# Loading the second Wq quarter directly behind the first, with two x tiles and their transposes one step later

## The chip, the cores and the metric

The kernel runs on one core of a Trainium2 chip. The metric is the device time of one execution in microseconds. A figure for a kernel is the median of its runs, all with a granted TensorE clock of 1.0. The span is what the hardware profile of one execution covers; it is about 2 us shorter than the time of the same execution.

Some words used throughout: in this kernel TensorE does the matrix products and transposes and writes them to the memory called PSUM; ScalarE copies results out of PSUM (a *cast* is such a copy of a finished product into bf16); VectorE does the statistics and the normalisations. A load *lands* when its data have arrived.

## The reference

Two layers, each of windowed attention and a feed-forward block, on 2048 tokens of width 1024 in bf16:

```
for _ in range(2):
    x = x + attention(layernorm(x), wqkv, wo)      # 32 heads, window 8, dilation 2
    x = x + gelu(layernorm(x) @ w1 + b1) @ w2 + b2 # F = 3584
```

Only the very start matters for this change: the layer norm of the first 512 tokens and their product with Wq, the first third of wqkv.

## The kernel before

The kernel works in groups of 512 tokens, that is four x tiles of 128 tokens. For the first group it must fetch both x and Wq before TensorE can do anything useful, so it fetches Wq in four quarters (each two of the eight 128-row blocks of the contraction) and starts with x tiles 0 and 1 alone. I call this *the first half*: Wq for tokens 0 to 255. *The second half* is Wq for tokens 256 to 511, from x tiles 2 and 3.

```python
load_x(0, 0, 2)                                  # x tiles 0 and 1
wq_first = [wpool.tile([P, KD // 2, D], BF16, name="wt") for _ in range(2)]
for k in range(0, KD, 2):
    load_wq_piece(wq_first[k // (KD // 2)], k)   # one quarter, 512 KB
    if k < 4:
        load_x(0, 2 + k // 2, 3 + k // 2)        # x2 behind quarter 1, x3 behind quarter 2
# ... cut ...
def transpose_on_pe(xn, out, pst=None, parts=None):
    # ... cut ...
    for k in range(KD):                          # eight 128x128 transposes into PSUM
        pe(nc.tensor.transpose(pst[:, k, :], xn[:, k * P:(k + 1) * P], ident[:]))
    parts = parts or [act.copy]                  # then a copy from PSUM to xnT
    # ... cut ...
# in ln_first(), with VectorE and ScalarE held to program order
    both = psum.tile([P, 2, KD, P], BF16, name="L", bufs=1)
    # ... x tiles 0 and 1 ...
    stats(2)
    stats(3)                                     # statistics on VectorE, sqrt on ScalarE
    for tt in range(2, 4):
        first_late.append((norm(tt), xa[0][:, tt, :, :], both[:, tt - 2, :, :]))
    # ... cut ...
# in gen_qkv(), n == 0
first = {}
for kq in range(4 if n == 0 else 0):             # Wq quarters
    for c in range(6):                           # six output chunks, six PSUM accumulators
        first[c] = qkv_chunk(wq, c, xnT, first.get(c), kq * (KD // 4), (kq + 1) * (KD // 4), 0, 2)
        if (kq, c) in ((2, 5), (3, 5)):          # x2's, then x3's transposes
            for done in range(2 if kq == 3 else 0):
                act.copy(qT[:, done, 0:2 * P], first[done][:, 0:2 * P])
            transpose_on_pe(*first_late.pop(0))
for c in list(first)[2:]:
    act.copy(qT[:, c, 0:2 * P], first[c][:, 0:2 * P])
for c in range(6 if n == 0 else NCH, NCH):       # chunks 6 and 7
    ps = qkv_chunk(wq, c, xnT, t0=0, t1=2)
    act.copy(qT[:, c, 0:2 * P], ps[:, 0:2 * P])
for c in range(NCH):                             # the second half
    t0 = 2 if n == 0 else 0
    ps = qkv_chunk(wq, c, xnT, t0=t0)
    act.copy(qT[:, c, t0 * P:], ps[:, t0 * P:])
    yield
```

TensorE's order is the program's. The order on the other engines and on the load queue is chosen by a scheduler, except where the program pins it. A half of the tile `both` is 2 KB in each partition.

Of the kernel before, what the change touches and what calls it, by code (L numbers as in the profile page):

```python
# [17 lines left out]
def kernel(  # L18
# [18 lines left out]
    P = 128  # L37
# [41 lines left out]
    def acc_tile():  # L79
        return psum.tile([P, T], F32, name="acc", bufs=6)  # L80
# [23 lines left out]
    vec, act, pool, sp = InOrder(nc.vector), InOrder(nc.scalar), InOrder(nc.gpsimd), InOrder(nc.sync)  # L104
# [6 lines left out]
    def pe(inst):  # L111
        if last_pe[0] is not None:
            dep_order(inst, last_pe[0], "PE program order")
        last_pe[0] = inst
        return inst

    def mm(*args, **kwargs):
        return pe(nc.tensor.matmul(*args, **kwargs))  # L118
# [3 lines left out]
    def load_x(g, t0=0, t1=NTT):  # L122
        for tt in range(t0, t1):
            t = g * NTT + tt
            sp.dma_start(x[t][:], x_in[t * P:(t + 1) * P, :])

    def load_qkv(which):
        tiles = []
        for h in range(2):
            wt = wpool.tile([P, KD // 2, D], BF16, name="wt")  # L130
            sp.dma_start(wt[:], wqkv_v[:, h * (KD // 2):(h + 1) * (KD // 2), which * D:(which + 1) * D])
            tiles.append(wt)
        return tiles

    def load_wq_piece(wt, k):
        sp.dma_start(wt[:, k % (KD // 2):k % (KD // 2) + 2, :], wqkv_v[:, k:k + 2, 0:D])
# [2 lines left out]
    wq_first = [wpool.tile([P, KD // 2, D], BF16, name="wt") for _ in range(2)]  # L139
    for k in range(0, KD, 2):  # L140
        load_wq_piece(wq_first[k // (KD // 2)], k)
        if k < 4:
            load_x(0, 2 + k // 2, 3 + k // 2)

    warm = bigp.tile([P, P], BF16, name="big")
    vec.memset(warm[:], 0.0)
# [68 lines left out]
    def transpose_on_pe(xn, out, pst=None, parts=None):  # L215
        if pst is None:
            pst = psum.tile([P, KD, P], BF16, name="acc", bufs=6)
        for k in range(KD):
            pe(nc.tensor.transpose(pst[:, k, :], xn[:, k * P:(k + 1) * P], ident[:]))  # L219
        parts = parts or [act.copy]  # L220
        n = KD // len(parts)
        for h, copy in enumerate(parts):
            copy(out[:, h * n:(h + 1) * n, :], pst[:, h * n:(h + 1) * n, :])
# [8 lines left out]
    first_late = []  # L232
# [51 lines left out]
    def qkv_chunk(wts, c, xnT, ps=None, k0=0, k1=KD, t0=0, t1=NTT):  # L284
        if ps is None:
            ps = acc_tile()
        for k in range(k0, k1):
            mm(ps[:, t0 * P:t1 * P], lhsT=wts[k // (KD // 2)][:, k % (KD // 2), c::NCH], rhs=xnT[:, t0:t1, k, :],
               start=(k == 0), stop=(k == KD - 1), skip_group_check=t1 - t0 < NTT)
        return ps  # L290
# [16 lines left out]
    def new_prod(n, c):  # L307

        s = st[n]
        prod = bigp.tile([P, NTT, W, P], BF16, name="big")  # L310
        q = s["qT"][:, c, :].rearrange("p (b t) -> p b t", t=P)
        vec.tensor_tensor(out=prod[:], in0=q.unsqueeze(2).to_broadcast([P, NTT, W, P]), in1=win_by_tile(s["kT"][:, c, :]), op=ALU.mult)
        tree = s["prods"]
        tree.append(prod)
        if c % 2 == 1:
            for _ in range(1 if c % (NCH // s["parts"]) == 1 else 2):
                b = tree.pop()
                vec.tensor_tensor(out=tree[-1][:], in0=tree[-1][:], in1=b[:], op=ALU.add)

    def gen_qkv(n, parts=1, defer=False, qk_pool=None, v_late=False, qk_next=None):  # L320
        g = n % NG
        xnT = xa.pop(n)
        s = st[n]
        s["parts"] = parts
        s["prods"] = []
        qk_pool = qk_pool or attp
        wq = wq_first if n == 0 else load_qkv(0)
        wk = load_qkv(1)
        if n == 0:
            early_tiles = ln_early((1, None), (2, qk_next))  # L330
            for _ in range(NTT):
                next(early_tiles)
            wv = load_qkv(2)
            for _ in early_tiles:
                pass
            load_x(3)
        qT = qk_pool.tile([P, NCH, T], BF16, name="qT")
        first = {}
        for kq in range(4 if n == 0 else 0):
            for c in range(6):  # L340
                first[c] = qkv_chunk(wq, c, xnT, first.get(c), kq * (KD // 4), (kq + 1) * (KD // 4), 0, 2)
                if (kq, c) in ((2, 5), (3, 5)):
                    for done in range(2 if kq == 3 else 0):
                        act.copy(qT[:, done, 0:2 * P], first[done][:, 0:2 * P])
                    transpose_on_pe(*first_late.pop(0))
        for c in list(first)[2:]:
            act.copy(qT[:, c, 0:2 * P], first[c][:, 0:2 * P])
        for c in range(6 if n == 0 else NCH, NCH):
            ps = qkv_chunk(wq, c, xnT, t0=0, t1=2)
            act.copy(qT[:, c, 0:2 * P], ps[:, 0:2 * P])  # L350
        for c in range(NCH):
            t0 = 2 if n == 0 else 0
            ps = qkv_chunk(wq, c, xnT, t0=t0)
            act.copy(qT[:, c, t0 * P:], ps[:, t0 * P:])
            yield
        if n > 0 and not v_late:
            wv = load_qkv(2)
        kT = qk_pool.tile([P, NCH, HALO + T], BF16, name="kT")
        s["qT"], s["kT"] = qT, kT
        act.on = n > 2  # L360
        act.copy(kT[:, :, 0:HALO], (zhalo if g == 0 else khalo)[:])
        act.on = False
        for c in range(NCH):
            ps = qkv_chunk(wk, c, xnT)
            act.copy(kT[:, c, HALO:], ps[:])
            if not defer:
                new_prod(n, c)
            yield
        if g + 1 < NG:
            act.copy(khalo[:], kT[:, :, T:T + HALO])  # L370
        vT = attp.tile([P, NCH, HALO + T], BF16, name="vT", bufs=2)
        s["vT"] = vT
        if v_late:
            wv = load_qkv(2)
        act.on = n > 2
        act.copy(vT[:, :, 0:HALO], (zhalo if g == 0 else vhalo)[:])
        act.on = False
        for c in range(NCH):
            ps = qkv_chunk(wv, c, xnT)
            act.copy(vT[:, c, HALO:], ps[:])  # L380
            yield
        if g + 1 < NG:
            act.copy(vhalo[:], vT[:, :, T:T + HALO])
# [163 lines left out]
    def ln_early(*groups):  # L547

        tiles = []
        for n, pool in groups:  # L550
            xa[n] = new_xnT(pool)
            xns = bigp.tile([P, NTT, D], BF16, name="big") if pool is None else pool.tile([P, NTT, D], BF16, name="qT")
            tiles += [(n * NTT + tt, xns[:, tt, :], xa[n][:, tt, :, :]) for tt in range(NTT)]
        vec.on = True
        ahead = ln_stats(tiles[0][0])
        for i, (t, xn, xT) in enumerate(tiles):
            mv_rstd = ahead
            if i + 1 < len(tiles):
                ahead = ln_stats(tiles[i + 1][0])
            ln_norm(t, *mv_rstd, xn)  # L560
            sp.dma_start_transpose(xT, xn.rearrange("s (k p) -> s k p", p=P))
            if i + 1 == len(tiles):
                vec.on = False
            yield
# [28 lines left out]
    with tc.tile_pool(name="early", bufs=1) as early:  # L593
        load_x(1)
        load_x(2)
        stage(gen_qkv(0, qk_next=early), sides=at(14, load_b2))
        q1 = gen_qkv(1, defer=True, qk_pool=early)
        stage(q1, sides=at(6, attend, 0) + at(6, spread, 0) + at(6, hold) + each(new_prod, 1, 8, 1, 0, 4) + each(av, 0, 12, 1))
        q2 = gen_qkv(2, defer=True)
        stage(q2, 18)  # L600
        new_prod(1, 4)
        hold()
        stage(gen_wo(0))
        hold()
        stage(q2, sides=each(new_prod, 1, 0, 1, 5, 8))
# [15 lines left out]
    n = N - 2  # L621
# [35 lines left out]
```

## Time and profile before

Six runs: median 1232.87 us, 1232.72 to 1234.22 (three of them, with the median 1233.37, were known when the prediction was made). The profiled run has a span of 1230.8 us. Two lines of its page: the busy time of each engine with its share of the span, and the chain of work that ended last, by engine.

```profile
PE 1222.2 (99%) x5739; PEld 632.6 (51%) x5789; DVE 861.9 (70%) x922; ACT 307.3 (25%) x491; POOL 87.2 (7%) x207
...
PE 99%; DMA 1%; issue 0%; SPq 0%; DVE 0%
```

TensorE is the bottleneck, and the chain is TensorE nearly all the way. So a change can win only what TensorE waits, and loses whatever wait it adds. TensorE's timeline at the start shows that wait. The columns are start in us, length in us, engine, source line, operation, output and inputs, number of instructions, and in brackets the idle time before and what ended it.

```profile
8.92 2.81 PE L118 MATMUL acc<-xnT,wt 128*128 128x256 bf16 x24
12.06 1.53 PE L118 MATMUL acc<-xnT,wt 128*128 128x256 bf16 x12 [0.33 <-DMA wt<-in_A_wqkv_dram]
13.43 0.61 PE L219 MATMUL L<-ident,xn 128*128 128x128 bf16 x8
13.88 1.48 PE L118 MATMUL acc<-xnT,wt 128*128 128x256 bf16 x12
15.20 0.61 PE L219 MATMUL L<-ident,xn 128*128 128x128 bf16 x8
15.64 1.59 PE L118 MATMUL acc<-xnT,wt 128*128 128x256 bf16 x13
```

The 8.92 line is quarters 1 and 2, the 12.06 line is quarter 3 after a 0.33 us wait for its load, then x2's transposes, quarter 4, x3's transposes, and from 15.64 chunks 6 and 7 and everything after. One reading trap: a matmul of this shape is listed with 273 ns (the profile models where it ends), but the next starts 109 ns later.

VectorE in the same stretch (statistics of x2, of x3, then the two normalisations):

```profile
8.89 1.28 DVE L93 BATCH_NORM_STATS2 stats<-x 128x6 f32<-128x512 bf16 x2
...
10.69 1.29 DVE L93 BATCH_NORM_STATS2 stats<-x 128x6 f32<-128x512 bf16 x2 [0.28 <-DMA x<-in_A_x_dram]
...
12.28 0.55 DVE L93 TENSOR_SCALAR xn<-x,mv,rstd 128x1024 bf16<-128x1024 bf16 x1
...
12.94 0.55 DVE L93 TENSOR_SCALAR xn<-x,mv,rstd 128x1024 bf16<-128x1024 bf16 x1
```

ScalarE: x2's copy out of PSUM, casts of finished accumulators, x3's copy.

```profile
14.08 1.01 ACT L93 COPY xnT<-L 128x1024 bf16<-128x1024 bf16 x1 [1.11 <-PE L L219]
14.99 1.21 ACT L93 CAST qT<-acc 128x256 bf16<-128x256 f32 x4
16.04 1.07 ACT L93 COPY xnT<-L 128x1024 bf16<-128x1024 bf16 x1
```

x3's copy runs from 16.04 to 17.11 us, while TensorE works on chunks 6 and 7. By counting records, the second half starts at 17.40 us (its first matmul is the 81st record after 64 matmuls and 16 transposes, beginning with the first Wq matmul), so the copy is hidden.

### The profile page before, as it was taken

How to read it: one execution, taken by the hardware profiler on the slowest of the kernel's cores; microseconds unless marked ns; L12 is line 12 of the kernel's file. 1: busy time of each engine (PE TensorE's matmuls, PEld its weight loads, DVE VectorE, ACT ScalarE, POOL GpSimd, SP SyncE). 2: the span in 40 equal slices, each digit the busy share in tenths (PEclk: the TensorE clock that was granted, in tenths of full speed). 3: DMA queues.
4: the chain of work that ended last, by engine and by line, in shares of the span. 5: the costliest groups of instructions: out<-in, count | busy, mean ns of one | idle time of the engine just before them, and what ended most of it. 6: DMA issues, size and time to landing. Idle time of an engine off the chain costs nothing.

```text
span 1230.8 us, 13962 instructions
## 1 busy us (share of the span) xinstructions
PE 1222.2 (99%) x5739; PEld 632.6 (51%) x5789; DVE 861.9 (70%) x922; ACT 307.3 (25%) x491; POOL 87.2 (7%) x207
## 2 busy tenths in 40 slices
PE   9999999999999999999999999999999999999998
PEld 7666544456444564445544465444654444444444
DVE  7989899988998599375993759937599797011001
ACT  4343152014320143202431024310244101400310
POOL 3010010010010000100011000010000002000000
PEclk9999999999999999999999999999999999999999
DMA  9954665656556654856447565486664558446441
GB/s 290 300 179 143 182 222 185 201 154 209 181 165 215 180 162 163 229 172 186 150 163 238 171 171 170 158 223 202 171 196 145 188 196 208 151 158 196 155 135 52
DMA packets 219391, 225.06 MB, mean 183 GB/s; under 512 B 68194, under 2 KB 187136, under 8 KB 217024
## 3 DMA queue, kind: packets, MB, share of 16 engines
q1 hardware_dynamic: 214704, 208.69, 55.5%
q0 software_dynamic: 4624, 15.49, 3.3%
q8 instruction: 45, 0.74, 0.2%
q14 instruction: 18, 0.15, 0.0%
HBM read 191.11 MB, written 4.72 MB: 159 GB/s over the span
## 4 chain that ended last, share of the span: by engine, by line
PE 99%; DMA 1%; issue 0%; SPq 0%; DVE 0%
PE acc L118 98%; DMA wt<-in_A_wqkv_dram 1%; SPq L93 0%; PE L L118 0%; PE L L219 0%; DVE x L93 0%
## 5 line engine op out<-in xcount | busy, mean ns | idle before, releaser
L118 PE MATMUL acc<-xnT,wt 128*128 128x512 bf16 (+1 forms) x3392 | 720.9, 375 | 0.4 <-DMA wt<-in_A_wqkv_dram 0.3
L118 PEld LDWEIGHTS <-wt 128*128 128x128 bf16 x3392 | 400.5, 119 | 319.1 <-issue 1.4
L118 PE MATMUL acc<-wt,hT 128*128 128x512 bf16 (+1 forms) x1780 | 386.0, 376 | 2.1
L118 PEld LDWEIGHTS <-hT 128*128 128x128 bf16 x1820 | 178.1, 98 | 208.9
L93 DVE TENSOR_TENSOR big<-big 128x1024 bf16<-128x1024 bf16 (+2 forms) x184 | 245.2, 1360 | 2.2
L93 ACT ACTIVATE hT<-acc,b1T 128x512 bf16<-128x512 f32 x224 | 152.7, 688 | 332.3 <-PE acc L118 332.1
L93 DVE TENSOR_TENSOR big<-qT,kT 128x4096 bf16<-128x4096 bf16 x64 | 143.8, 2286 | 48.4 <-ACT kT L93 47.8
L93 DVE TENSOR_TENSOR big<-abc,vT 128x4096 bf16<-128x4096 bf16 x64 | 144.7, 2286 | 14.0 <-DMA abc<-a 13.4
L93 DVE TENSOR_TENSOR tmp<-acc,b2bc 128x512 f32<-128x512 f32 x56 | 38.6, 690 | 146.7 <-PE acc L118 143.7
L93 ACT CAST qT<-acc 128x512 bf16<-128x512 f32 (+1 forms) x72 | 38.0, 545 | 351.1 <-PE acc L118 351.1
L118 PE MATMUL acc<-wt,oT 128*128 128x512 bf16 x440 | 97.4, 379 | 0.4
L93 DVE BATCH_NORM_STATS2 stats<-x 128x6 f32<-128x512 bf16 x128 | 85.6, 682 | 4.5 <-DMA x<-in_A_x_dram 3.4
L118 PEld LDWEIGHTS <-oT 128*128 128x128 bf16 x448 | 43.8, 98 | 52.8
L93 DVE TENSOR_TENSOR x<-acc,big 128x512 bf16<-128x512 f32 (+1 forms) x9 | 5.7, 633 | 90.0 <-PE acc L118 90.0
L93 ACT CAST vT<-acc 128x512 bf16<-128x512 f32 x64 | 37.5, 586 | 83.3 <-PE acc L118 83.3
L93 ACT CAST kT<-acc 128x512 bf16<-128x512 f32 x64 | 37.4, 587 | 67.0 <-PE acc L118 67.0
L93 POOL TENSOR_TENSOR rstd<-mv,eps_t 128x1 f32<-128x1 f32 x56 | 14.2, 253 | 515.4 <-DVE mv L93 509.4
L93 DVE TENSOR_TENSOR x<-acc,x 128x512 bf16<-128x512 f32 x64 | 42.9, 671 | 4.8 <-PE acc L118 4.4
L93 DVE TENSOR_SCALAR xn<-x,mv,rstd 128x1024 bf16<-128x1024 bf16 x52 | 28.4, 547 | 20.2 <-POOL rstd L93 20.1
L93 DVE TENSOR_TENSOR x<-tmp,x 128x512 bf16<-128x512 f32 x56 | 38.7, 690 | 1.3
L93 POOL DMA_DIRECT2D big<-big x24 | 13.3, 565 | 256.3 <-DVE big L93 237.6
L93 POOL TENSOR_TENSOR rstd<-rstd,mhalf 128x1 f32<-128x1 f32 x56 | 31.0, 553 | 4.4
(68 smaller groups left out, 228.8 us busy)
## 6 DMA issues: line engine op xcount, KB each, us to landing
wt<-in_B_w_dram SPq DMA_DIRECT2D x56, 1024.0 KB, 5.7
wt<-in_B_w_dram SPq DMA_DIRECT2D x64, 896.0 KB, 4.9
wt<-in_A_wqkv_dram SPq DMA_DIRECT2D x46, 1024.0 KB, 5.6
wt<-in_A_wo_dram SPq DMA_DIRECT2D x16, 1024.0 KB, 5.0
big<-big POOLq DMA_DIRECT2D x24, 256.0 KB, 3.6
abc<-a POOLq DMA_DIRECT2D x24, 256.0 KB, 5.3
x<-in_A_x_dram SPq DMA_DIRECT2D x16, 256.0 KB, 6.2
out_dram<-x SPq DMA_DIRECT2D x31, 128.0 KB, 2.1
```

Source lines behind the costliest of these rows:

```text
L93: inst = f(*args, **kwargs)
L118: return pe(nc.tensor.matmul(*args, **kwargs))
```

## The change

The intent is to remove the wait for quarter 3: quarter 2 is loaded directly behind quarter 1, x2 and x3 move one quarter back in the queue, and since they land later, their transposes move back too: x2's into the middle of quarter 4, x3's behind chunks 6 and 7.

```diff
     for k in range(0, KD, 2):
         load_wq_piece(wq_first[k // (KD // 2)], k)
-        if k < 4:
-            load_x(0, 2 + k // 2, 3 + k // 2)
+        if 0 < k < 6:
+            load_x(0, 1 + k // 2, 2 + k // 2)
@@
                 first[c] = qkv_chunk(wq, c, xnT, first.get(c), kq * (KD // 4), (kq + 1) * (KD // 4), 0, 2)
-                if (kq, c) in ((2, 5), (3, 5)):
-                    for done in range(2 if kq == 3 else 0):
-                        act.copy(qT[:, done, 0:2 * P], first[done][:, 0:2 * P])
+                if (kq, c) == (3, 2):
                     transpose_on_pe(*first_late.pop(0))
-        for c in list(first)[2:]:
+        for c in list(first)[:3]:
             act.copy(qT[:, c, 0:2 * P], first[c][:, 0:2 * P])
         for c in range(6 if n == 0 else NCH, NCH):
-            ps = qkv_chunk(wq, c, xnT, t0=0, t1=2)
-            act.copy(qT[:, c, 0:2 * P], ps[:, 0:2 * P])
+            first[c] = qkv_chunk(wq, c, xnT, t0=0, t1=2)
+        if n == 0:
+            transpose_on_pe(*first_late.pop(0))
+        for c in list(first)[3:]:
+            act.copy(qT[:, c, 0:2 * P], first[c][:, 0:2 * P])
```

## The prediction

> **What bounds the kernel.** TensorE. The page gives PE busy 1222.2 of 1230.8 us (99%), and the chain of waits is 98% the matmul helper. It touches only the first 18 us, where a merged timeline shows three PE waits: 1.05 us for the memset, 1.50 us for the first normalised tile (matmuls resume at 7.15), and 0.33 us for the third Wq quarter (11.73 to 12.06). The first two stay. After 12.06 no PE wait is listed, so PE time won or lost before reaches the end unabsorbed.
>
> **What changes.** Nothing is added or removed: same matmuls, transposes, copies, DMAs, reordered. Landings before (issue plus time to landing): Wq quarter 1 at 7.9, x2 8.6, quarter 2 10.0, x3 10.7, quarter 3 12.0, quarter 4 13.35 us. They land in issue order, about 0.67 us per x tile and 1.35 per quarter. That agrees with the Trainium skill, "DMA: Bandwidth & Descriptors", section "Two DMAs through the same engine are not ordered": descriptors of one queue start in order but are pipelined. Estimated landings after: quarter 2 9.3, x2 10.0, quarter 3 11.35, x3 12.0, quarter 4 still 13.35.
>
> PE after, by 0.114 us per 128x256 matmul step:
> - Quarters 1 and 2 run 8.92 to 11.7, quarter 3 without a wait to 13.1: the 0.33 us wait is gone.
> - PE then waits about 0.25 us for quarter 4 (13.35). The wait is moved, not removed.
> - DVE runs in program order and normalises x2 only after the statistics of x3, which start at 12.05 instead of 10.69 us; xn2 is ready at 14.2 (before 12.83). PE reaches x2's transposes after six matmuls at 14.05: another 0.15 us wait.
> - Transposes (0.45), six matmuls, 16 matmuls of chunks 6 and 7: to about 17.2; x3's transposes to 17.65.
> - The next instruction, the first matmul over token tiles 2 and 3, reads all of xnT tile 3, which ScalarE still has to copy out of PSUM. Before, chunks 6 and 7 (1.83 us of PE) stood between and hid the copy; now nothing does. PSUM drain and semaphore 0.2 to 0.4, copy 1.01 to 1.07 us in the trace. ScalarE's order also puts chunk 7's qT cast (0.37 us) ahead of it. PE waits about 1.5 us (17.65 to 19.15).
>
> Sum, all critical: -0.33 +0.25 +0.15 +1.5, about +1.6 us (first matmul of the second half at 17.47 before, about 19.1 after).
>
> **Prediction.** 1233.37 + 1.6 = about 1235.0 us; 8 in 10: 1233.4 to 1236.6. Runs of before spread by 1.3 us. Faster by over 2%: 0.005; within 2%: 0.985; slower by over 2%: 0.01.
>
> **What would show it right or wrong.** A PE wait of 1.2 to 1.8 us released by ScalarE's xnT copy near 17.7; no wait at quarter 3; a wait of 0.1 to 0.4 at quarter 4; x2's stats starting near 10.0 and x3's near 12.0; quarter 4 landing still near 13.35; DVE's start on x4 moving from 14.07 to about 14.8, harmless since PE moves more; the span past 20 us otherwise equal, shifted.
>
> **What would make it wrong.** ScalarE slower to reach x3's copy (casts stacking behind the late square root and x2's copy), up to +1 us more; a PE wait for a free accumulator at chunk 6; landings that don't follow bytes in issue order; another chip's base; a wait further on, invisible now, that absorbs the shift (then about 1233.4), or a DVE shift of 0.7 us reaching a head sum.

## The result, and the profile after

Median 1234.30 us of six runs (1233.88 to 1234.89), against 1232.87 before: +1.4 us. The ratio of the mean time of the changed kernel's fast runs to that of the fast runs of before in the same rounds is 1.001, with an interval of 0.9997 to 1.0023. (Ratios are computed so throughout, so they are not quite the ratios of the medians.) The interval includes 1, so the times alone show no difference. The traces do, one profiled run of each kernel. The span is 1232.2 us.

TensorE's timeline after, answering to the one above:

```profile
8.79 4.13 PE L118 MATMUL acc<-xnT,wt 128*128 128x256 bf16 x36
13.45 0.88 PE L118 MATMUL acc<-xnT,wt 128*128 128x256 bf16 x6 [0.52 <-DMA wt<-in_A_wqkv_dram]
14.26 0.62 PE L219 MATMUL L<-ident,xn 128*128 128x128 bf16 x8
14.71 2.57 PE L118 MATMUL acc<-xnT,wt 128*128 128x256 bf16 x22
17.12 0.61 PE L219 MATMUL L<-ident,xn 128*128 128x128 bf16 x8
18.83 5.40 PE L118 MATMUL acc<-xnT,wt 128*128 128x256 bf16 x48 [1.10 <-ACT xnT L93]
```

The first line now is quarters 1, 2 and 3 without a break: the wait for quarter 3 is gone. Quarter 4 is split in two by x2's transposes (14.26), and is waited for (0.52). Chunks 6 and 7 come before x3's transposes (17.12). Then TensorE stands still until 18.83. All waits of TensorE in the whole run, with total, number and longest:

```profile
PE acc L118 <- ACT xnT L93: 1.1, 1, 1.1
PE acc L118 <- DVE big L93: 1.1, 1, 1.1
PE acc L219 <- DVE xn L93: 0.7, 1, 0.7
PE acc L118 <- DMA wt<-in_A_wqkv_dram: 0.5, 1, 0.5
```

The two waits in the middle are the start-up (the kernel before has them too, 1.1 and 1.5 us). The first is new, and the last, for quarter 4, stands in place of the 0.3 us for quarter 3. VectorE and ScalarE, the same pieces as above:

```profile
10.03 1.29 DVE L93 BATCH_NORM_STATS2 stats<-x 128x6 f32<-128x512 bf16 x2 [1.18 <-DMA x<-in_A_x_dram]
...
12.06 1.28 DVE L93 BATCH_NORM_STATS2 stats<-x 128x6 f32<-128x512 bf16 x2 [0.50 <-DMA x<-in_A_x_dram]
...
13.65 0.55 DVE L93 TENSOR_SCALAR xn<-x,mv,rstd 128x1024 bf16<-128x1024 bf16 x1
```

```profile
15.04 1.03 ACT L93 COPY xnT<-L 128x1024 bf16<-128x1024 bf16 x1
...
17.32 0.37 ACT L93 CAST qT<-acc 128x256 bf16<-128x256 f32 x1 [0.16 <-PE acc L118]
17.77 1.01 ACT L93 COPY xnT<-L 128x1024 bf16<-128x1024 bf16 x1
```

x3's statistics start at 12.06 instead of 10.69 us, and since VectorE was told to do them before x2's normalisation, x2's is done at 14.20 instead of 12.83 us. x3's copy runs from 17.77 to 18.78, and TensorE resumes 0.05 us later.

The idle time in brackets counts from the listed end of the last matmul, so it is about 0.16 us less than what TensorE lost. Start to start, TensorE lost 0.68 us at quarter 4, 0.10 us at x2's transposes and 1.26 us behind x3's: 2.04 us, against 0.49 before. That is 1.55 us more between the first Wq matmul and the second half. In this profile the first Wq matmul came 0.13 us earlier (8.79 for 8.92), because x0, the first load of all, landed 0.13 us earlier (3.42 for 3.54 us); nothing in the change explains that. 1.55 less 0.13 is 1.42 us, and the spans differ by 1.4. From the second half's first matmul to the last matmul both kernels take the same, 1210.06 and 1210.05 us. So the whole result lies in these ten microseconds.

This gives a sharper measure than the time. For each run I quote, from the records of its profile: the start of the first Wq matmul, the start of the second half, the difference of the two (called *the stretch*), and *the rest*, from there to the start of the last matmul.

| kernel | first Wq matmul | second half | stretch | rest | span | median time | before, same rounds |
|---|---|---|---|---|---|---|---|
| before | 8.92 | 17.40 | 8.48 | 1210.06 | 1230.8 | 1232.87 | |
| changed | 8.79 | 18.83 | 10.04 | 1210.05 | 1232.2 | 1234.30 | 1232.87 |
| loads_only | 8.90 | 18.15 | 9.25 | 1210.11 | 1231.6 | 1233.53 | 1232.90 |
| places_only | 9.06 | 18.25 | 9.18 | 1210.05 | 1231.6 | 1233.94 | 1232.90 |
| x3_before_chunks | 9.07 | 18.59 | 9.52 | 1210.06 | 1232.0 | 1234.10 | 1232.90 |
| copy_in_four | 8.82 | 18.02 | 9.20 | 1210.30 | 1231.6 | 1233.82 | 1232.90 |
| casts_behind | 8.94 | 18.20 | 9.26 | 1210.17 | 1231.7 | 1233.76 | 1232.95 |
| norm2_first | 9.35 | 19.53 | 10.18 | 1210.17 | 1233.0 | 1235.00 | 1232.95 |
| loads_norm2 | 8.98 | 18.66 | 9.68 | 1210.86 | 1232.8 | 1234.42 | 1232.95 |
| x3_later_norm2 | 8.92 | 17.09 | 8.17 | 1210.37 | 1230.8 | 1232.97 | 1232.95 |
| two_tiles | 8.96 | 18.05 | 9.09 | 1210.25 | 1231.6 | 1233.69 | 1232.85 |
| best2 | 8.96 | 16.89 | 7.93 | 1211.44 | 1231.7 | 1233.33 | 1232.85 |
| loads_norm2_pool | 8.91 | 18.00 | 9.09 | 1211.02 | 1232.3 | 1234.48 | 1232.85 |
| best3 | 9.10 | 17.03 | 7.93 | 1210.39 | 1230.7 | 1232.85 | 1233.12 |

Read it with care: the first Wq matmul starts anywhere from 8.79 to 9.35 us. In all fourteen profiles it starts 5.37 to 5.38 us after x0 lands, so this spread is the spread of one landing (3.42 to 3.97 us), which no edit touches. When loads land late in a run, the waits for them grow as well, and there is one profile of each kernel. The twelve experiments ran beside runs of the kernel before. Single runs of that kernel spread from 1232.23 to 1234.63 us. A difference in time below about half a us says nothing here; a wait in the trace with its releaser does.

### The profile page after: what moved, and what is told of

Its sections match the earlier page's. It is cut to its first block, busy times and chain, and to the rows that moved or that the text cites. A ratio compares the mean times of both kernels' runs of the same rounds, so it can differ in the third digit from the quotient of the medians.

```text
span 1232.2 us, 13962 instructions
## 1 busy us (share of the span) xinstructions
PE 1223.2 (99%) x5739; PEld 632.8 (51%) x5789; DVE 861.6 (70%) x922; ACT 306.9 (25%) x491; POOL 86.9 (7%) x207
## 4 chain that ended last, share of the span: by engine, by line
PE 98%; DMA 1%; SPq 0%; issue 0%; ACT 0%; DVE 0%
PE acc L118 98%; DMA wt<-in_A_wqkv_dram 1%; SPq L93 0%; PE L L118 0%; ACT xnT L93 0%; PE L L219 0%; DVE x L93 0%
```

## The experiments

My theory was that of the prediction: the loss is the sum of a wait for ScalarE's copy of x3, which the new place of the transposes uncovers, a wait for quarter 4, and a small one for x2's normalisation. The first rival: the load order itself is what costs, and the places of the transposes are harmless.

### One part of the change at a time

**loads_only**: the kernel before with the new load order alone.

```diff
-        if k < 4:
-            load_x(0, 2 + k // 2, 3 + k // 2)
+        if 0 < k < 6:
+            load_x(0, 1 + k // 2, 2 + k // 2)
```

> The kernel before with the new load order alone; transposes and casts stay where they were. My theory (the chain x3 landing, x3 statistics, x2 normalisation gates x2's transposes, and the placement hides ScalarE's copy): no PE wait for quarter 3, but PE reaches x2's transposes at about 12.8 us and xn2 is ready only at about 14.25, so one PE wait of about 1.3 us released by DVE xn; no wait for quarter 4 and none for ScalarE. About +0.9 us on before, 1233.8. Rival (the loads alone make the loss, because quarter 4 is waited for 0.5 us and the rest is a later start of everything): +1.4 us with a wait for quarter 4.

1233.53 us, 0.6 above before by the medians, ratio 1.0003 (0.9991 to 1.0016). TensorE's timeline, quarters 1 to 3 and x2's transposes:

```profile
8.90 4.12 PE L118 MATMUL acc<-xnT,wt 128*128 128x256 bf16 x36
14.18 0.62 PE L219 MATMUL L<-ident,xn 128*128 128x128 bf16 x8 [1.15 <-DVE xn L93]
```

No wait for quarter 3 or 4, and one for x2's normalisation, 1.15 us. This is as the theory had it. Start to start, x2's transposes lose 1.32 us at the old place, against 0.10 in the changed kernel; but there the wait for quarter 4 (0.68) is added. So by these figures, moving x2's transposes back saved some 0.5 us of what the later loads cost.

**places_only**: the changed kernel with the load order of before (the reverse of that edit).

> The changed kernel with the old load order: only the transposes and casts are moved. My theory: the wait for quarter 3 is back (0.33 us in the list of waits), no wait for quarter 4, none for x2's transposes, and the wait of about 1.1 us for ScalarE's copy of x3 stays. About +1.2 us on before, 1234.1. Rival (the loads make the loss): equal to before.

1233.94 us, 1.0 above before, ratio 1.0011 (0.9998 to 1.0025). The start of the second half on TensorE:

```profile
18.25 8.01 PE L118 MATMUL acc<-xnT,wt 128*128 128x256 bf16 x68 [1.10 <-ACT xnT L93]
```

The wait for ScalarE's copy is 1.10 us, as in the changed kernel, with the old loads. So the places alone cost this wait, and the rival falls. One part of the expectation failed: the wait for quarter 3 did not come back. Its load was issued at 3.70 us and landed 7.8 us later, at 11.5, where in the profile of before it was issued at 3.69 and landed 8.3 us later, at 12.0. The two loads in the list of DMA issues (number, KB, us to landing), before and places_only:

```profile
wt<-in_A_wqkv_dram SPq DMA_DIRECT2D x1, 512.0 KB, 8.3
...
wt<-in_A_wqkv_dram SPq DMA_DIRECT2D x1, 512.0 KB, 7.8
```

The wait that the change set out to remove is itself not there in every run.

### The place of x3's transposes

**x3_before_chunks**: the changed kernel, x3's transposes ahead of chunks 6 and 7.

```diff
+        if n == 0:
+            transpose_on_pe(*first_late.pop(0))
         for c in list(first)[:3]:
             act.copy(qT[:, c, 0:2 * P], first[c][:, 0:2 * P])
@@
-        if n == 0:
-            transpose_on_pe(*first_late.pop(0))
```

> The changed kernel with x3's transposes moved ahead of chunks 6 and 7 again, all else kept. My theory: chunks 6 and 7 (1.8 us of PE) hide the copy, so the ScalarE wait of 1.1 us goes entirely; the waits for quarter 4 (0.5) and for xn2 (0.1) stay. About 1.25 us less than the changed kernel, +0.25 us on before, 1233.1. Rival: if the wait were due to ScalarE's late casts and not to the placement, 0.5 us or more of it would stay.

1234.10 us: by time no better than the changed kernel. The expectation failed, although the 1.1 us wait did go: the stretch is 0.52 us shorter where 1.25 was expected. TensorE (the rest of quarter 4, then x3's transposes) and ScalarE (three casts, then x2's copy):

```profile
14.99 0.83 PE L118 MATMUL acc<-xnT,wt 128*128 128x256 bf16 x6
16.39 0.61 PE L219 MATMUL L<-ident,xn 128*128 128x128 bf16 x8 [0.57 <-ACT xnT L93]
```

```profile
14.52 0.91 ACT L93 CAST qT<-acc 128x256 bf16<-128x256 f32 x3
15.31 1.03 ACT L93 COPY xnT<-L 128x1024 bf16<-128x1024 bf16 x1
```

A wait that no earlier run had: x3's *transposes* now wait 0.57 us for ScalarE. x3's data are not the reason (its normalisation ended at 15.13 us). The transposes start 0.05 us after x2's copy ends (15.31 + 1.03 = 16.34). x2's and x3's transposes write the two halves of one PSUM tile, and a write to the tile waits for the read of it. Looking back, the kernel before has x2's copy ending at 15.09 and x3's transposes at 15.20 us: the same guard, hidden behind quarter 4's twelve matmuls.

**copy_in_four**: the changed kernel with x3's copy in four pieces.

```diff
         if n == 0:
-            transpose_on_pe(*first_late.pop(0))
+            transpose_on_pe(*first_late.pop(0), parts=[act.copy] * 4)
```

> The changed kernel with x3's PSUM copy cut into four ScalarE copies of 256 columns, so that the first matmuls of the second half need only the first piece. My theory: the PE wait shrinks from 1.1 us to about 0.4 us, plus about 0.2 us in small waits between the pieces, since a piece takes about 0.32 us and its two matmuls 0.22. About 0.4 to 0.6 us less than the changed kernel, 1233.8. If the wait is not for the copy's length but for the transposes or ScalarE's casts before it, nothing is won.

1233.82 us. The start of the second half on TensorE:

```profile
18.02 8.19 PE L118 MATMUL acc<-xnT,wt 128*128 128x256 bf16 x68 [0.46 <-ACT xnT L93]
```

The wait is 0.46 us instead of 1.10, and start to start it fell from 1.26 to 0.62 us. That is 0.64 us less, just what the first piece is shorter than the whole copy (0.37 us for 1.01): the length of the copy is the wait. The rest grew by 0.25 us, 0.18 of it in three waits between the pieces. In all that is 0.4 us won, the lower end of what was expected.

### What holds x3's transposes

**casts_behind**: as x3_before_chunks, with ScalarE pinned to take x2's copy ahead of the casts. TensorE's order is the same.

```diff
+        act.on = n == 0
@@
+        for c in list(first)[:2]:
+            act.copy(qT[:, c, 0:2 * P], first[c][:, 0:2 * P])
         if n == 0:
             transpose_on_pe(*first_late.pop(0))
-        for c in list(first)[:3]:
+        for c in list(first)[2:6]:
             act.copy(qT[:, c, 0:2 * P], first[c][:, 0:2 * P])
@@
-        for c in list(first)[3:]:
+        for c in list(first)[6:]:
@@
+        act.on = False
```

> x3's transposes ahead of chunks 6 and 7 as in the run before this, and ScalarE's order changed so that x2's copy comes straight behind x2's transposes and the qT casts behind it; TensorE's order is the same, instruction for instruction. My reading of the failed expectation: x3's transposes write the same PSUM tile that x2's copy still reads, and three casts (0.9 us) in front of that copy made them wait 0.57 us. If so that wait goes, and the 1.1 us wait for x3's copy stays away; left are the waits for quarter 4 (0.3 to 0.5) and xn2 (0.1): +0.2 to +0.4 us on before, about 1233.2, with the second half starting 8.8 us after the first Wq matmul (8.5 before, 10.05 in the changed kernel). Rival (moving x3's transposes cannot help, ScalarE is simply short of time): a ScalarE wait of 0.5 us or more shows up elsewhere.

1233.76 us. x2's copy came earlier, and yet, on TensorE and on ScalarE:

```profile
16.00 0.61 PE L219 MATMUL L<-ident,xn 128*128 128x128 bf16 x8 [0.44 <-ACT xnT L93]
```

```profile
14.93 1.01 ACT L93 COPY xnT<-L 128x1024 bf16<-128x1024 bf16 x1 [0.57 <-PE L L219]
```

The wait is 0.44 us; I had expected it to go. The casts were not the cause, only an addition. The copy starts at once behind x2's transposes and takes 1.01 us, and only six matmuls (0.66 us) stand between the two sets of transposes. Again x3's start 0.06 us after the copy's end.

**two_tiles**: as casts_behind, the transposes into two PSUM tiles of one bank each. The PSUM space is given back to the tile `L` after the first group.

```diff
-        both = psum.tile([P, 2, KD, P], BF16, name="L", bufs=1)
+        both = [tpool[0].tile([P, KD, P], BF16, name=f"T{i}") for i in range(2)]
@@
-            first_late.append((norm(tt), xa[0][:, tt, :, :], both[:, tt - 2, :, :]))
+            first_late.append((norm(tt), xa[0][:, tt, :, :], both[tt - 2]))
# cut: tpool is a PSUM pool of its own, opened before and closed after the first group;
# L then comes from a new pool in its place
```

> The run with the casts moved behind x2's copy (transposes of x3 ahead of chunks 6 and 7), with one more edit: the transposes of x2 and x3 go to two PSUM tiles of their own instead of two halves of one tile. In every run so far x3's transposes began 0.05 to 0.1 us after x2's copy ended. Theory: the wait is the guard of the shared tile; with two tiles the 0.44 us wait goes and x3's transposes follow the six matmuls or xn3 at once. Second half starts about 8.7 us after the first Wq matmul (9.26 with one tile): about 1233.2. Rival (TensorE waits for xn3 or for ScalarE's engine itself): the wait stays, or moves to chunk 6.

1233.69 us. TensorE (x3's transposes, then chunks 6 and 7) and ScalarE (x2's copy):

```profile
15.43 0.61 PE L219 MATMUL T<-ident,xn 128*128 128x128 bf16 x8
16.30 9.97 PE L118 MATMUL acc<-xnT,wt 128*128 128x256 bf16 x85 [0.27 <-ACT qT L93]
```

```profile
14.97 1.01 ACT L93 COPY xnT<-T 128x1024 bf16<-128x1024 bf16 x1 [0.57 <-PE T L219]
```

x3's transposes now start at 15.43, in the middle of x2's copy (14.97 to 15.98), without a wait. That settles the shared tile as the cause of the wait at the transposes. Most of the gain was lost again, as the rival had it: chunk 6 waits 0.27 us in the list for the cast that frees an accumulator, because that cast now stands behind x2's copy. The stretch fell only from 9.26 to 9.09, not to 8.7. In this order ScalarE is short of time.

The Trainium skill, "PSUM — Partial Sum Buffer", section "PSUM bank collisions raise a hardware error", asks for guards by bank and quadrant, not by address. The same page, section "Specifications (TRN2)", gives a bank as 2 KiB in each partition, so the two halves lay in different banks and the guard here was wider than that page asks for. This run, with one tile per bank, was correct and free of that wait.

### VectorE's order, and ScalarE's

**norm2_first**: the changed kernel, x2 normalised before x3's statistics.

```diff
-        stats(2)
-        stats(3)
         for tt in range(2, 4):
+            stats(tt)
             first_late.append((norm(tt), xa[0][:, tt, :, :], both[:, tt - 2, :, :]))
```

> The changed kernel with x2 normalised before the statistics of x3 on VectorE. If xn2's lateness is VectorE's program order, the 0.1 us wait at x2's transposes goes and nothing else: second half starts about 9.9 us after the first Wq matmul instead of 10.05, 1234.2, not to be told from the changed kernel by time. If the loads themselves made xn2 late, nothing changes.

1235.00 us of four runs (ratio 1.0017, 1.0003 to 1.0030), the slowest of all. The small wait at x2's transposes did go: they start at 14.71 us, 0.72 us after the start of the six matmuls before them, which is six steps of 0.11 us and a little. But the wait for x3's copy grew from 1.10 to 1.36 us, so the stretch is 10.18 us where 9.9 was expected. x3's square root on ScalarE now comes behind x2's normalisation (14.81 us), x2's copy and the casts stack up behind it, and ScalarE reaches x3's copy only at 18.39 us, 0.22 us after x3's transposes ended (18.17). In this run x0 also took 3.17 us to land where it took 2.74 in the profile of before, which nothing in the edit explains, so its time is not to be read as the edit's cost.

**loads_norm2**: loads_only with the same edit.

> The new load order with the old places of the transposes (the loads-alone run) and x2 normalised before x3's statistics. Theory: xn2 is ready at about 12.6 us, just before TensorE comes to it at 12.8, so the 1.15 us wait of the loads-alone run goes; x2's transposes then fill most of the time until quarter 4 lands, leaving 0.1 to 0.2 us of wait. Second half starts about 8.3 us after the first Wq matmul (8.5 before): -0.2 us on before, 1232.7, the best of all, though times spread by more than that. Rival (the loads are bad in themselves): still +0.5 us or more.

1234.42 us (1233.93 to 1235.66): it failed, and this was to be the best of all. TensorE (x2's transposes, x3's transposes) and ScalarE (x3's square root, x2's copy):

```profile
13.38 0.62 PE L219 MATMUL L<-ident,xn 128*128 128x128 bf16 x8
...
16.47 0.61 PE L219 MATMUL L<-ident,xn 128*128 128x128 bf16 x8 [0.91 <-ACT xnT L93]
```

```profile
14.85 0.29 ACT L93 ACTIVATE std<-mv,eps_t 128x1 f32<-128x1 f32 x1 [2.31 <-DVE mv L93]
...
15.41 1.00 ACT L93 COPY xnT<-L 128x1024 bf16<-128x1024 bf16 x1
```

x2's transposes end at 14.00 us, and x2's copy starts at 15.41. In front of it on ScalarE stands the square root of x3's variance, which waits for x3's statistics; these were now put behind x2's normalisation, and the loads landed some 0.7 us later in this run than in loads_only (quarter 3 at 11.95 for 11.29, for which TensorE waited 0.20 us in the list). x3's transposes wait for that copy through the shared tile. The Trainium skill, "TensorE: Matmul & The Clock Gate", in its table of specifications, calls ScalarE's and VectorE's queues strict FIFO; that is what shows here: ScalarE stood idle for 2.31 us until the square root at 14.85, the last 0.85 us of it with x2's copy ready to run.

**loads_norm2_pool**: the same with x3's deviation on GpSimd, so that ScalarE has nothing of x3 to wait for.

```diff
         stats(2)
         first_late.append((norm(2), xa[0][:, 2, :, :], both[:, 0, :, :]))
+        first_late.append((ln_norm(3, *ln_stats(3)), xa[0][:, 3, :, :], both[:, 1, :, :]))
@@
+    build_constants()
     ln_first()
-    build_constants()
```

(The first two lines replace the loop of loads_norm2; its turn for x3 is gone.)

> The run that failed (new load order, old places, x2 normalised first: TensorE waited 0.91 us for x2's copy), with x3's reciprocal deviation computed on GpSimd instead of ScalarE. Theory: ScalarE takes its instructions in order, and x3's square root, waiting for x3's statistics, stood in front of x2's copy. Then x2's copy now starts within 0.2 us of the end of x2's transposes (1.4 us after it in the failed run), and the PSUM wait of 0.91 us goes; x3's transposes then wait for xn3 instead, which comes about 0.4 us later than with ScalarE, so TensorE still waits 0.2 to 0.8 us there, with DVE xn as its releaser. Second half at about 9.0 to 9.4 us after the first Wq matmul (9.68). Rival (late loads alone): x2's copy as late as before.

1234.48 us of four runs (1233.40 to 1236.34). ScalarE (x2's copy) and TensorE (both sets of transposes):

```profile
13.52 1.01 ACT L93 COPY xnT<-L 128x1024 bf16<-128x1024 bf16 x1 [1.15 <-PE L L219]
```

```profile
12.87 0.61 PE L219 MATMUL L<-ident,xn 128*128 128x128 bf16 x8
...
15.79 0.62 PE L219 MATMUL L<-ident,xn 128*128 128x128 bf16 x8 [0.77 <-DVE xn L93]
```

x2's copy starts at 13.52, 0.04 us after x2's transposes end (12.87 + 0.61): the square root was what held it. The wait is now for x3's normalisation, 0.77 us, as expected, and the stretch of 9.09 us is in the expected range. The time gained nothing: VectorE was later, and the first sum over heads near 65 us waited 0.6 us for it.

### The versions that the runs point to

**x3_later_norm2**: as loads_norm2, but only x3 is moved back in the load queue.

```diff
-        if 0 < k < 6:
-            load_x(0, 1 + k // 2, 2 + k // 2)
+        if k in (0, 4):
+            load_x(0, 2 + k // 4, 3 + k // 4)
```

> As the last, but x2 loaded where it was (behind quarter 1) and only x3 one quarter later. Theory: no wait for quarters 2 and 3, xn2 ready at about 11.2 us, more than a us ahead of need, and the same small wait for quarter 4: the same as the last within 0.1 us in the trace. If quarter 2 (landing near 10.0 us, needed near 10.1) is late in this order, a wait of up to 0.2 us shows there instead.

1232.97 us against 1232.95: the same as before. The trace shows the stretch at 8.17 us, 0.31 better than before, with no wait for any quarter in the list; the small wait expected for quarter 4 did not come. The shared tile shows once more, in x3's transposes on TensorE and x2's copy on ScalarE:

```profile
14.89 0.61 PE L219 MATMUL L<-ident,xn 128*128 128x128 bf16 x8
```

```profile
13.85 1.00 ACT L93 COPY xnT<-L 128x1024 bf16<-128x1024 bf16 x1
```

The transposes start 0.04 us after the copy ends, and start to start they lost 0.25 us, too little for the list of waits. The rest is 0.31 us longer.

**best2**: that, with two PSUM tiles and ScalarE's order pinned (x2's copy, two casts, x3's copy, the other casts).

> What the runs point to: x3 alone loaded one quarter later, x2 normalised before x3's statistics, transposes in their old places, two PSUM tiles, ScalarE's order fixed as in the old kernel. Theory: no TensorE wait at all from the first Wq matmul on: second half starts 7.8 to 7.95 us after it (8.17 with one tile, 8.48 before). About -0.5 us on before, 1232.4, which the spread of the times may hide. Rival: ScalarE's square root of x3 holds x2's copy up so that chunk 6 or the second half waits 0.2 us or more.

1233.33 us. The stretch is 7.93 us, 0.55 better than before and without a wait, as expected; the 0.24 us that it is shorter than in x3_later_norm2 fit the wait at the shared tile. But the rest is 1.4 us longer. TensorE near 53 us, in the first Wq product of the second token group:

```profile
53.70 6.48 PE L118 MATMUL acc<-xnT,wt 128*128 128x512 bf16 x29 [1.01 <-DMA wt<-in_A_wqkv_dram]
```

The second half of that group's Wq, a load of 1 MB, was not there in time. It is issued behind four loads of x for a group that comes much later. Most of this is not the gain at the start: the load landed at 53.65 us, in the profile of before at 52.01. The matmul that needs it would have been due at 52.52 us, where in before it started at 52.88. So of the 1.17 us lost start to start, 0.36 come from being earlier, and by these figures the other 0.8 would have been lost with such a late landing in the kernel before too. loads_norm2, which won nothing at the start, also lost 0.55 us there (landing at 54.65).

**best3**: best2 with the call for these x loads moved behind the next group's Wq and Wk; the scheduler then put three of the four behind that Wq.

```diff
             for _ in early_tiles:
                 pass
-            load_x(3)
+        if n == 1:
+            load_x(3)
```

> The last combined kernel won 0.55 us at the start and lost 1.0 us at 52.7 us, waiting for the second half of group 1's Wq, which is issued behind four loads of x for group 3 that nobody needs before 100 us. This run is the same with three of these four x loads moved behind that Wq load. Theory: the wait sat in the load queue; Wq's second half now lands about 2 us earlier, the 1.0 us wait goes, and the start's gain reaches the end: span 1230.2 to 1230.8 by the profile (1231.7 before this edit), about 1232.4 us, 0.4 to 0.6 under the kernel before. Rival: the late Wq is set by something earlier (the DMA transposes ahead of it, or a weight buffer not yet free), and a wait of 0.5 us or more stays.

1232.85 us against 1233.12 in the same rounds, ratio 0.9996 (0.9982 to 1.0010). TensorE, from chunk 6 on and at the first sum over heads:

```profile
15.28 48.62 PE L118 MATMUL acc<-xnT,wt 128*128 128x256 bf16 x264
64.08 0.62 PE L118 MATMUL L<-big,smat 128*32 128x512 bf16 x8 [0.19 <-DVE big L93]
```

The wait at 53 us is gone (that load was issued at 41.67 us instead of 43.27 and landed at 50.22): one line of 264 instructions runs from 15.28 to 63.90. The next limit shows at 64 us, 0.19 us for VectorE. The span is 1230.7 us for 1230.8 before. By the trace it wins 0.37 us up to the second half (0.55 in the stretch, less 0.18 of a later start) and gives back most of it further on. I cannot claim it as faster.

## Why the prediction was right

- **The size and the sign.** Predicted 1235.0 us with 1233.4 to 1236.6; measured 1234.30. As a difference, +1.6 predicted from a base of 1233.37, and +1.4 measured from 1232.87. That the sum is so close is luck: start to start, the four terms below miss by -0.16, +0.43, -0.05 and -0.24 us, and these misses cancel. The signs, the largest term and the releasers are not luck.
- **The removed wait.** Quarter 3 is no longer waited for. I took 0.33 us for it from the list of waits; start to start it was 0.49. places_only shows that it depends on when the load lands in a run.
- **The moved wait.** Quarter 4 was predicted to cost 0.25 us and cost 0.52 in the list, 0.68 start to start: the worst-sized term. It landed at 13.40 us, 13.35 predicted, so the landing was right. The step of 0.114 us per matmul was too large (36 matmuls at 0.110), TensorE started 0.13 us earlier, and so it was ready near 12.8 us instead of 13.1.
- **x2's normalisation.** Predicted ready at 14.2 us with a wait of 0.15; measured 14.20 and 0.10. loads_only shows what the same lateness costs at the old place: 1.15 us. norm2_first shows that it is VectorE's order, since with the other order this wait goes.
- **The uncovered copy.** Predicted 1.5 us, measured 1.10 in the list and 1.26 start to start. (In the list, this wait and quarter 4's both lie outside what the prediction had named as its signs, 1.2 to 1.8 and 0.1 to 0.4 us.) places_only has it with the old loads, copy_in_four shortens it by cutting the copy, and x3_before_chunks removes it by moving the transposes. ScalarE's cast of chunk 7 hardly delayed it: it ended at 17.69 us, just as x3's transposes did (17.73).
- **Nothing absorbs it.** The rest is 1210.05 us in the changed kernel and 1210.06 before, as predicted. That is one loss in one pair of profiles. Time won did not all reach the end: best2's 0.55 us met a load at 53 us that landed late, and best3 gave back 0.33 of the same 0.55 us after the start.
- **What I had missed, and what did not matter here.** The guard of the shared PSUM tile doesn't appear in the prediction. ScalarE's late square root appears only among what would make it wrong, with casts and x2's copy stacking behind it; norm2_first then showed that. In the changed kernel x2's copy ends at 16.07 us and x3's transposes come at 17.12, so neither is felt. They decided four of the experiments (x3_before_chunks, casts_behind, norm2_first, loads_norm2).

What stays open: why the same load lands at different times from profile to profile. x0, the first in the queue and issued at 0.80 us each time, landed anywhere from 3.42 to 3.97 us. Nor does one profile of each kernel tell how much of this is the kernel and how much the run.

## What to carry to other kernels

When transposes or any other producer on the bottleneck engine are moved later, look at what stood between them and their first user: it was hiding the copy in between, and that must be costed before the wait that the move removes. Draw the first twenty microseconds as chains of load, statistics, normalisation, transposes and copy for each tile, and include the order on the helper engines and the guards of shared tiles, since one instruction that waits holds up everything queued behind it. In these runs a loss at the start was paid in full, while a gain of half a microsecond had to pass the next limits (a load at 53 us, VectorE at 64 us) before it could reach the end.

## What the Trainium skill lacked or had wrong

- "PSUM — Partial Sum Buffer", section "PSUM bank collisions raise a hardware error", says to guard by bank. I found nothing on what a guard wider than that costs: a tile over two banks made TensorE wait 0.44 us for a read of the other bank (casts_behind), and one tile per bank took that wait away (two_tiles).
- "TensorE: Matmul & The Clock Gate": I found nothing, there or on the other pages that I read, on how the length listed for a pipelined matmul hides part of a wait: 273 ns listed for a step of 109 ns, so that a wait of 0.49 us is listed as 0.33.
- "DMA: Bandwidth & Descriptors", section "Two DMAs through the same engine are not ordered", says that descriptors in one queue of one DMA engine start in order but are pipelined; landings of the first group's loads here followed the order of issue. I found nothing there on the spread from run to run at a kernel's start: the third quarter landed at 12.0 us in the kernel before and at 11.5 in places_only, with the same loads ahead of it, and quarter 1, always issued at 1.72 us as the third load, landed anywhere from 6.55 to 8.58 us in the fourteen profiles.
